# One decode kernel, four small edits at once: where the identity is built, the first POOL instruction, the row layout of two weights, and the last attention pair

## The chip, the cores and the metric

The kernel runs on one NeuronCore of a Trainium2 chip. The metric is the device time of one execution in microseconds (us). Times of the same kernel on the same chip differ by one to five microseconds from run to run, which is as much as the parts of this change are worth. So the study leans on two instruments: timed runs (five or six of each later kernel, means compared) and stretches inside the traces that are much steadier than the total.

## The reference, cut to what matters

Eight sequences decode one token through two layers. Each layer is attention with a cache of 4096 keys and values, then a small network. Of the first norm's "mixer" only the residual remains at sequence length 1, so B_w1 and B_w2 are never read.

```python
B, Sq, D = 8, 1, 448;  Hq, Hkv, Sk, Dh = 16, 8, 4096, 256;  F = 1792
def A(x, k_cache, v_cache, wq, wo):
    q = (x @ wq) -> [B, Hq, 1, Dh]
    scores = q @ k^T * Dh**-0.5          # each kv head serves 2 query heads
    o = softmax(scores) @ v
    return o.reshape(B, 1, Hq * Dh) @ wo
def Bl(x, ...):                          # what is left of it for S = 1
    return x + gelu(layernorm(x) @ w3) @ w4
x = A_x
for layer in range(2):                   # same weights and caches in both layers
    x = x + A(layernorm(x), ...)
    x = x + Bl(layernorm(x), ...)
```

The caches are 134 MB each. The kernel streams both in layer 1, and in layer 2 streams the values and those keys that it could not keep on the chip: 472 MB in all.

## The kernel before

Five buffers of 1 MB form a ring. SyncE issues one load when a buffer comes free. TensorE turns keys by a matmul with the identity, VectorE and ScalarE copy them out of PSUM (where matmuls leave their results), TensorE forms scores; POOL sums over partitions. A helper records every operation with what it reads and writes, so a line number in the profile is that of the call. Of a matmul's two operands the stationary one is loaded first and held (a weight load in the profile), and the moving one is streamed past it.

```python
# start: the identity, which every transpose needs
op("pool", lambda e: e.memset(ident[:, :], 0.0), writes=[r_ident])
op("pool", lambda e: e.affine_select(out=ident[:, :], in_=ident[:, :], compare_op=ALU.not_equal,
                                     fill=1.0, base=0, pattern=[[-1, P]], channel_multiplier=1), ...)
op("dve", lambda e: e.tensor_copy(ident4[:, :], ident[:, :]), ...)
...
# 448 rows = 3 chunks of 128 and one of 64: the 64 rows are stored as two half-width pieces,
# the lower columns on partitions 0-63, the upper on 64-127
def load_rows(t, tf, src, name):
    w = src.shape[1] // 2
    for kc in range(1, KC):
        parts.append((t[:, kc - 1, :], src[row0(kc):row0(kc + 1), :]))
    for half in range(2):
        parts.append((tf[64 * half:64 * half + 64, :], src[0:64, w * half:w * half + w]))
...
# wo (after the first pair) and w4: one 896-byte row to a partition and a packet
A_wo.rearrange("(t m) n -> m t n", m=P)
...
def pv(g, a):                             # probabilities times values, half a pair
    for i in range(HALF):                 # probabilities are the stationary operand (128 x 2)
        e.matmul(pvb[at:at + 2, 0:DH], pT[q][0][:, a * HALF + i, :], v[:, i, :], ...)
    if a == 1:
        op("dve", lambda e: e.tensor_copy(ob[:, :], pvb[:, 0:DH]), ...)
def finish(g):                            # turn the result: two transposes, a sum of 4 parts, a scale
    e.transpose(pvb[:, ...], ob[:, c * P:(c + 1) * P], ident4[:, :]) ...
    op("dve", tensor_reduce(os_, ...)); op("dve", tensor_tensor(oT[...], os_, 1 / sum, ALU.mult))
...
def rsqrt(src, dst, n):                   # integer first guess, three Newton steps: 11 VectorE operations
...
g = len(seq) - 1                          # the end
finish(g - 1); pv(g, 0); pv(g, 1); finish(g); drain()      # drain: output projection, norm, network
op("dve", lambda e: e.tensor_copy(xo[:, :, :], xT[:, :, :]), ...)
```

## Time and profile before

| | before |
|---|---|
| time, median of 3 runs | 1171.94 us |
| span of the profiled run | 1170.8 us |
| DMA queue of the kernel's loads | 98.4% of 16 engines' span |
| TensorE / VectorE / ScalarE / POOL busy | 80 / 42 / 27 / 9% |
| start of the last value matmuls to the end | 15.3 us |

From the page of the kernel before: the busy line of TensorE, the DMA share and the rate in 40 equal slices (tenths; GB/s), and the queue line (packets, MB, share).

```profile
PE 937.4 (80%) x19304; PEld 816.5 (70%) x19304; DVE 488.2 (42%) x1792; ACT 312.8 (27%) x891; POOL 105.4 (9%) x281
...
DMA  9999999999999999999999999999999999999994
GB/s 346 384 416 420 418 405 416 421 418 420 399 421 420 419 414 413 410 420 418 411 408 418 419 418 405 420 420 405 415 418 420 404 419 411 418 416 399 399 411 166
...
q1 hardware_dynamic: 70496, 471.97, 98.4%
```

DMA is busy in every slice but the last. The rate is about 420 GB/s where it is good, 346 and 384 in the first two slices (29 us each), and dips to around 400 in some later ones. A kernel like this has only two places where time can be won: stretches in which the stream is slow, and the work that is left when the last values have come.

The start, from the timeline of the kernel before (columns: start us, busy us, engine, line, operation, output and inputs, count, idle time before and what ended it).

```profile
11.19 0.28 POOL L204 TENSOR_SCALAR_AFFINE_SELECT ident<-ident 128x128 bf16<-128x128 bf16 x1 [10.27 <-issue]
...
11.84 5.86 PE L601 MATMUL tk<-ident,ring 128*128 128x128 f32 x32
...
21.35 0.44 POOL L350 PARTITION_ALL_REDUCE sg<-sm  x1 [9.87 <-issue]
...
22.25 0.26 PE L412 MATMUL mm<-lnT,wq_sb 128*128 128x24 bf16 x3 [4.56 <-DVE lnT L378]
```

POOL idles for 10.27 us before its first real instruction and 9.87 us before the first sum, with no other engine to blame ("issue"). The profile does not show what it waits for; the prediction takes it for a load of code, and "wait for code" below is this reading. Nothing can be transposed before 11.5 us.

The same trace by stretches (columns: stretch, length, busy time and count of TensorE, weight loads, VectorE, ScalarE, POOL, then granted clock, DMA share, GB/s; a share above 1 means that packets overlap).

```profile
11.00:15.00 4.00, 3.47 (x19) 3.44 (x20) 2.56 (x13) 0.59 (x1) 0.28 (x1) 1.00 1.02 432
15.00:19.00 4.00, 2.70 (x19) 2.46 (x17) 0.39 (x1) 1.76 (x3) 0.00 (x0) 1.00 1.09 247
32.00:41.00 9.00, 7.40 (x138) 6.56 (x138) 3.88 (x11) 3.76 (x10) 1.06 (x3) 1.00 1.09 380
```

At 11 to 15 us full-width loads move at 432 GB/s. From 15 to 19 us the rate is 247 at a DMA share of 1.09: the engines are not idle, each packet takes longer. At 32 to 41 us it is wo's turn, at 380.

The tail, from the timeline, cut to the steps that the change touches.

```profile
1155.49 1.02 PE L699 MATMUL pvb<-ring,pT 128*2 128x256 bf16 x16 [0.63 <-DMA ring<-in_A_v_cache_dram]
1156.57 0.42 DVE L705 COPY ob<-pvb 128x256 f32<-128x256 f32 x1 [3.94 <-PE pvb L699]
...
1157.05 0.69 PE L717 MATMUL pvb<-ident,ob 128*128 128x128 f32 x2 [0.53 <-DVE ob L705]
1157.78 0.17 DVE L720 TENSOR_REDUCE os<-pvb 128x4 f32<-128x16 f32 x1 [0.65 <-PE pvb L717]
1157.99 0.18 DVE L724 TENSOR_TENSOR oT<-os,rc 128x4 bf16<-128x4 f32 x1
...
1158.22 0.83 PE L451 MATMUL mm<-oT,wo_sb 128*64 128x24 bf16 x16 [0.48 <-DVE oT L724]
...
1161.91 0.17 DVE L327 TENSOR_SCALAR smi<-sm 128x6 int32<-128x6 int32 x1
...
1163.92 0.17 DVE L337 SCALAR_TENSOR_TENSOR sm<-sm 128x6 f32<-128x6 f32 x1
...
1164.90 0.24 ACT L496 ACTIVATE hw<-hw 128x42 f32<-128x42 f32 x1 [13.57 <-DVE hw L494]
...
1167.84 0.18 DVE L768 CAST xo<-xx 128x32 bf16<-128x32 f32 x1
...
1169.14 0.31 SPq L779 DMA_DIRECT2D out_dram<-x_row  x1
```

From the last landing (1155.49, read here and below as the start of the matmuls that wait for it) to the output projection (1158.22) are 2.73 us; the inverse root is 1161.91 to 1164.15, just before the network's hidden layer needs it.

### The profile page before, as it was taken

The numbers are of one execution on the slowest core, as the hardware profiler recorded it, in microseconds if no ns is written. First come the engines' busy times: TensorE is split into PE (matmuls) and PEld (weight loads), VectorE is DVE, ScalarE is ACT, GpSimd is POOL, SyncE is SP. The second block draws the span as 40 slices with busy tenths as digits, with TensorE's granted clock in tenths as the row PEclk, the third lists the DMA queues.
The fourth block names the chain that finished last, engine by engine and source line by source line (L and its number), as shares of the span: only waits on it lengthen the run. The fifth ranks groups of instructions, "written<-read, shape, count | busy, mean of one in ns | idle before, by whom it ended". The sixth has DMA issues, their size and how long they took to land.

```text
span 1170.8 us, 42672 instructions
## 1 busy us (share of the span) xinstructions
PE 937.4 (80%) x19304; PEld 816.5 (70%) x19304; DVE 488.2 (42%) x1792; ACT 312.8 (27%) x891; POOL 105.4 (9%) x281
## 2 busy tenths in 40 slices
PE   4777898779877887778877888778887888889986
PEld 3666776668766776667766777667776777778774
DVE  2324543345334543345334543345333633354343
ACT  1223222223223232232223222223222322222230
POOL 0000001101010010000100010001000011000100
PEclk8879999999999999899989998999999999999996
DMA  9999999999999999999999999999999999999994
GB/s 346 384 416 420 418 405 416 421 418 420 399 421 420 419 414 413 410 420 418 411 408 418 419 418 405 420 420 405 415 418 420 404 419 411 418 416 399 399 411 166
DMA packets 70678, 474.70 MB, mean 405 GB/s; under 512 B 7248, under 2 KB 13280, under 8 KB 13792
## 3 DMA queue, kind: packets, MB, share of 16 engines
q1 hardware_dynamic: 70496, 471.97, 98.4%
q8 instruction: 151, 2.47, 0.9%
q14 instruction: 31, 0.25, 0.1%
HBM read 471.93 MB, written 0.01 MB: 403 GB/s over the span
## 4 chain that ended last, share of the span: by engine, by line
DMA 54%; PE 33%; DVE 8%; issue 4%; ACT 1%; POOL 1%; SPq 0%; POOLq 0%; DVEq 0%; ACTq 0%
DMA ring<-in_A_k_cache_dram 53%; PE tk L601 15%; PE ps L625 6%; PE pvb L699 5%; PE mm L451 3%; DVE ktr L608 2%; PE mm L412 1%; DMA ring<-in_A_v_cache_dram 1%; PE mm L515 1%; PE pvb L717 1%; DVE oT L724 1%; POOL gm L675 1%; DVE os L720 1%; DVE keep L608 1%; DVE ob L705 0%
## 5 line engine op out<-in xcount | busy, mean ns | idle before, releaser
L601 PE MATMUL tk<-ident,ring 128*128 128x128 f32 x2944 | 407.0, 290 | 138.8 <-DMA ring<-in_A_k_cache_dram 138.5
L601 PEld LDWEIGHTS tk<-ident,ring 128*128 128x128 f32 x2944 | 342.7, 148 | 184.7 <-DMA ring<-in_A_k_cache_dram 177.7
L608 DVE COPY ktr<-tk 128x512 f32<-128x512 f32 x224 | 153.9, 690 | 198.5 <-PE tk L601 198.1
L606 ACT COPY ktr<-tk 128x512 f32<-128x512 f32 x224 | 130.0, 586 | 310.1 <-PE tk L601 309.7
L699 PE MATMUL pvb<-ring,pT 128*2 128x256 bf16 x4096 | 160.0, 277 | 32.7 <-DMA ring<-in_A_v_cache_dram 23.9
L625 PE MATMUL ps<-qT,keep 128*128 128x48 bf16 x4608 | 160.2, 185 | 6.3 <-issue 3.8
L608 DVE COPY keep<-tk 128x512 f32<-128x512 f32 x144 | 99.5, 691 | 143.2 <-PE tk L601 141.9
L625 PEld LDWEIGHTS ps<-qT,keep 128*128 128x128 bf16 x4608 | 146.0, 98 | 16.1 <-issue 8.9
L606 ACT COPY keep<-tk 128x512 f32<-128x512 f32 x144 | 84.3, 586 | 257.1 <-PE tk L601 257.1
L681 ACT ACTIVATE pT<-ps,nb 128x32 bf16<-128x32 f32 x256 | 76.6, 299 | 260.0 <-DVE nb L677 213.2
L625 PE MATMUL ps<-qT,ktr 128*128 128x48 bf16 x3584 | 129.8, 183 | 10.0 <-ACT ktr L606 6.2
L625 PEld LDWEIGHTS ps<-qT,ktr 128*128 128x128 bf16 x3584 | 115.7, 97 | 20.6 <-ACT ktr L606 8.4
L675 POOL PARTITION_ALL_REDUCE gm<-pm x128 | 45.8, 357 | 782.7 <-DVE pm L672 782.7
L699 PEld LDWEIGHTS pvb<-ring,pT 128*2 128x2 bf16 x4096 | 76.2, 82 | 56.0 <-DMA ring<-in_A_v_cache_dram 28.5
L451 PE MATMUL mm<-oT,wo_sb 128*128 128x24 bf16 (+1 forms) x1408 | 64.1, 187 | 14.4 <-DVE oT L724 4.8
L705 DVE COPY ob<-pvb 128x256 f32<-128x256 f32 x128 | 53.8, 420 | 41.1 <-PE pvb L699 40.7
L451 PEld LDWEIGHTS mm<-oT,wo_sb 128*128 128x128 bf16 (+1 forms) x1408 | 51.5, 101 | 27.2 <-DVE oT L724 19.9
L686 POOL PARTITION_ALL_REDUCE dn<-rs x128 | 51.3, 401 | 151.0 <-ACT pT L681 151.0
L672 DVE TENSOR_REDUCE pm<-ps 128x2 f32<-128x64 f32 x128 | 28.7, 224 | 74.7 <-PE ps L625 74.1
L717 PE MATMUL pvb<-ident,ob 128*128 128x128 f32 x256 | 53.1, 290 | 6.9 <-DVE ob L705 6.9
L412 PE MATMUL mm<-lnT,wq_sb 128*128 128x24 bf16 x864 | 47.8, 184 | 5.2 <-DVE lnT L378 4.6
L412 PEld LDWEIGHTS mm<-lnT,wq_sb 128*128 128x128 bf16 x864 | 39.4, 98 | 14.8 <-issue 6.4
(68 smaller groups left out, 479.0 us busy)
## 6 DMA issues: line engine op xcount, KB each, us to landing
ring<-in_A_v_cache_dram SPq DMA_DIRECT2D x256, 1024.0 KB, 10.3
ring<-in_A_k_cache_dram SPq DMA_DIRECT2D x184, 1024.0 KB, 10.7
wo_sb<-in_A_wo_dram SPq DMA_DIRECT2D x1, 3584.0 KB, 25.0
wq_sb<-in_A_wq_dram SPq DMA_DIRECT2D x3, 1024.0 KB, 11.7
w_sb<-in_B_w_dram SPq DMA_DIRECT2D x1, 1568.0 KB, 18.2
w_sb<-in_B_w_dram SPq DMA_DIRECT2D x3, 448.0 KB, 16.0
wqf_sb<-in_A_wq_dram SPq DMA_DIRECT2D x2, 256.0 KB, 15.5
w3f_sb<-in_B_w_dram SPq DMA_DIRECT2D x2, 112.0 KB, 16.2
```

Of the source, the lines that this page charges most:

```text
L412: last = e.matmul(room(P, at + t * B, n), cols(kc, t), copies(rhs, n), start=(kc == 1), stop=(kc == 0), skip_group_check=True)
L451: last = e.matmul(room(w, C_P + c, 1), wo[:, t, row0(c):row0(c) + w], copies(oT[:, t // 2, t % 2, b:b + 1], 1), start=(t == 4 * h), stop=( ...
L601: last = e.transpose(bank[:, j * P:(j + 1) * P], src[:, 4 * (f % 4) + j, :].bitcast(f32), ident4[:, :])
L606: op("act", lambda e: e.copy(flat, bank[:, :]), reads=[r_bank], writes=[r_kt])
L608: op("dve", lambda e: e.tensor_copy(flat, bank[:, :]), reads=[r_bank], writes=[r_kt])
L625: last = e.matmul(pst[:, at:at + 2 * N_REP].rearrange("p (r j) -> p r j", j=2), kt(i, c), repeated(qT[:, b, c, 2 * h:2 * h + 2]), start=(c ...
L675: op("pool", lambda e: e.partition_all_reduce(gm[q][0][:, :], pm[q][0][:, :], P, ReduceOp.max), reads=[pm[q][1]], writes=[gm[q][1]])
L681: return e.activation(pT[q][0][:, :, :].rearrange("p i j -> p j i")[:, j, :], pst[:, C_S:C_S + 2 * NI].rearrange("p (i j) -> p j i", j=2)[ ...
L686: op("pool", lambda e: e.partition_all_reduce(dn[q][0][:, :], rs[q][0][:, :], P, ReduceOp.add), reads=[rs[q][1]], writes=[dn[q][1]])
L699: last = e.matmul(pvb[at:at + 2, 0:DH], pT[q][0][:, a * HALF + i, :], v[:, i, :], start=(a == 0 and i < 4), stop=(a == 1 and i >= HALF - 4 ...
L705: op("dve", lambda e: e.tensor_copy(ob[:, :], pvb[:, 0:DH]), reads=[r_pv], writes=[r_ob])
L717: last = e.transpose(pvb[:, DH + c * P:DH + (c + 1) * P], ob[:, c * P:(c + 1) * P], ident4[:, :])
```

## The change

Four edits. Identity: VectorE counts 0 to 31, turns that block and compares the two. POOL: its first instruction is a sum over partitions of zeros, so that the wait before POOL's first sum is over before a sum is needed. Rows: wo and w4 are stored with two consecutive rows on one partition (1792-byte packets); the columns of w3 and the order of the heads' elements follow (w3's 64 rows are now cut at column 1024, not 896), and wo is queued at the start. Tail: for the last pair the values are the stationary operand, so the result comes out already turned; the last 1 MB load is cut in two; the last inverse root is ScalarE's square root with its table loaded ahead; the result is written to the output tile directly.

```diff
-    op("pool", lambda e: e.memset(ident[:, :], 0.0), ...)
-    op("pool", lambda e: e.affine_select(out=ident[:, :], ...), ...)
-    op("dve", lambda e: e.tensor_copy(ident4[:, :], ident[:, :]), ...)
+    op("pool", lambda e: e.memset(sg[:, :], 0.0), writes=[r_sg])
+    op("pool", lambda e: e.partition_all_reduce(sg[:, :], sg[:, :], P, ReduceOp.add), ...)
+    for w in (1, 2, 4, 8, 16):                                   # count 0..31
+        op("dve", ... tensor_single_scalar(count[:, w:2 * w], count[:, 0:w], float(w), ALU.add), ...)
+    op("dve", lambda e: e.transpose(rows_, count), ...)
+    for p in range(0, P, 32):
+        op("dve", ... tensor_tensor(ident4[p:p+32, p:p+32], rows_[p:p+32], count[p:p+32], ALU.is_equal), ...)
...
-        lambda: op("sp", ... wo[:, :, :], A_wo.rearrange("(t m) n -> m t n", m=P) ...)    # after the first pair
+    op("sp", lambda e: e.dma_start(paired(wo), rows_of(A_wo)), ...)                       # at the start
+    def paired(t):   return t[:, :, :].rearrange("p (u c) n -> p u (c n)", c=2)
+    def rows_of(src): return src.rearrange("(u p c) n -> p u (c n)", p=P, c=2)
...
+        pieces = [(0, HALF, r)] if n < len(chunks) - 1 else [(0, HALF // 2, r), (HALF // 2, HALF, r_end)]
...
+    def rsqrt_end(src, dst, n):
+        op("act", lambda e: e.activation(w, v, ACT.Sqrt), ...)
+        table(ACT.Tanh)                       # a one-column activation that pulls the table back
+        op("dve", reciprocal) ... three more VectorE operations (one Newton step)
...
+    def close(g):
+        table(ACT.Sqrt)
+        for lo, hi in ((0, HALF), (HALF, HALF + HALF // 2), (HALF + HALF // 2, NI)):
+            for i in range(lo, hi):
+                for c in range(2):            # values stationary (128 x 128), probabilities moving
+                    e.matmul(tk[c][0][:, 0:48], v[:, i % HALF, c::2], repeated(pT[q][0][:, i, :]), ...)
+        for c in range(2):
+            op("dve", ... tensor_tensor(oT[:, 2*h:2*h+2, c, b], tk[c][0][:, 0:2], rc[q][0][:, :], ALU.mult), ...)
...
-    finish(g - 1); pv(g, 0); pv(g, 1); finish(g)
+    finish(len(seq) - 2)
+    while side: step()
+    close(len(seq) - 1)
...
-    op("dve", lambda e: e.tensor_copy(xo[:, :, :], xT[:, :, :]), ...)
+        to, r_to = (x_, r_x) if layer == 0 else (xo[:, :, lo:lo + n], r_xo)
```

More of the change, by code (lines that the diff above doesn't have):

```diff
@@ L15 @@
 NF = F // P
+F_LOW = 1024
 LN_EPS = 1e-5
@@ L151, in decode_two_layers @@
     w3, r_w3 = sb("w3_sb", [P, KC - 1, F], bf)
-    w3f = nc.alloc_sbuf_tensor("w3f_sb", [P, F // 2], bf)
+    w3f = nc.alloc_sbuf_tensor("w3f_sb", [P, F_LOW], bf)
     w4, r_w4 = sb("w4_sb", [P, NF, D], bf)
@@ L171, in decode_two_layers @@
     r_lift = Res()
+    r_table = Res()
     sm, r_sm = sb("sm", [P, 8, 2 * B], f32)
@@ L200, in decode_two_layers @@
     C_P = 448
-    op("pool", lambda e: e.memset(ident[:, :], 0.0), writes=[r_ident])
-    op("pool", lambda e: e.affine_select(out=ident[:, :], in_=ident[:, :],
-                                         compare_op=ALU.not_equal, fill=1.0, base=0,
-                                         pattern=[[-1, P]], channel_multiplier=1),
-       reads=[r_ident], writes=[r_ident])
-    op("dve", lambda e: e.tensor_copy(ident4[:, :], ident[:, :]), reads=[r_ident], writes=[r_ident4])
+    op("pool", lambda e: e.memset(sg[:, :], 0.0), writes=[r_sg])
+    op("pool", lambda e: e.partition_all_reduce(sg[:, :], sg[:, :], P, ReduceOp.add), reads=[r_sg], writes=[r_sg])
+    count, r_count = xc[:, :, :].rearrange("p c b -> p (c b)"), r_xc
+    rows_, r_rows = t1[:, :, :].rearrange("p c b -> p (c b)"), r_t1
+    op("dve", lambda e: e.memset(count[:, 0:1], 0.0), writes=[r_count])
+    op("dve", lambda e: e.memset(ident4[:, :], 0.0), writes=[r_ident4])
+    for w in (1, 2, 4, 8, 16):
+        op("dve", lambda e, w=w: e.tensor_single_scalar(count[:, w:2 * w], count[:, 0:w], float(w), ALU.add),
+           reads=[r_count], writes=[r_count])
+    op("dve", lambda e: e.transpose(rows_, count), reads=[r_count], writes=[r_rows])
+    for p in range(0, P, 32):
+        op("dve", lambda e, p=p: e.tensor_tensor(ident4[p:p + 32, p:p + 32], rows_[p:p + 32], count[p:p + 32],
+                                                 ALU.is_equal),
+           reads=[r_count, r_rows], writes=[r_ident4])
+    op("dve", lambda e: e.tensor_copy(ident[:, :], ident4[:, :]), reads=[r_ident4], writes=[r_ident])
     op("dve", lambda e: e.memset(pvb[:, :], 0.0), writes=[r_pv])
+    r_w3f = Res()
+    op("dve", lambda e: e.memset(w3f[64:P, F - F_LOW:F_LOW], 0.0), writes=[r_w3f])
     op("dve", lambda e: e.memset(xx[:, :, :, :], 0.0), writes=[r_x])
@@ L271, in decode_two_layers @@
     state = {"loaded": 0}
+    r_end = Res()
     def load_next():
@@ L279, in load_next, with load_rows @@
         t, r = ring[n % N_RING]
-        op("sp", lambda e: e.dma_start(
-            t[:, :, :], src[b, h].rearrange("(m s) d -> m s d", m=P)[:, a * HALF:(a + 1) * HALF, :]),
-           writes=[r], dma=f"ring{n % N_RING}")
+        pieces = [(0, HALF, r)] if n < len(chunks) - 1 else [(0, HALF // 2, r), (HALF // 2, HALF, r_end)]
+        r_end.w, r_end.r = r.w, list(r.r)
+        for k, (lo, hi, r_) in enumerate(pieces):
+            op("sp", lambda e, lo=lo, hi=hi: e.dma_start(
+                t[:, lo:hi, :], src[b, h].rearrange("(m s) d -> m s d", m=P)[:, a * HALF + lo:a * HALF + hi, :]),
+               writes=[r_], dma=f"ring{n % N_RING}" if k == 0 else "end")
     def row0(kc):
         return max(0, kc * P - 64)
-    def load_rows(t, tf, src, name):
+    def load_rows(t, tf, src, name, low):
         parts = []
-        w = src.shape[1] // 2
         for kc in range(1, KC):
             parts.append((t[:, kc - 1, :], src[row0(kc):row0(kc + 1), :]))
-        for half in range(2):
-            parts.append((tf[64 * half:64 * half + 64, :], src[0:64, w * half:w * half + w]))
+        parts.append((tf[0:64, 0:low], src[0:64, 0:low]))
+        parts.append((tf[64:P, 0:src.shape[1] - low], src[0:64, low:]))
         return [op("sp", lambda e, o=o, i=i: e.dma_start(o, i), writes=[Res()], dma=f"{name}{k}")
@@ L303, in reads_of, with paired, rows_of @@
         return out_
+    def paired(t):
+        return t[:, :, :].rearrange("p (u c) n -> p u (c n)", c=2)
+    def rows_of(src):
+        return src.rearrange("(u p c) n -> p u (c n)", p=P, c=2)
     op("sp", lambda e: e.dma_start(x_row[:, :], A_x[:, 0, :]), writes=[r_row], dma="x")
@@ L307, in decode_two_layers, with table @@
     load_next()
-    wq_r = reads_of(load_rows(wq, wqf, A_wq, "wq"))
+    wq_r = reads_of(load_rows(wq, wqf, A_wq, "wq", HQ * DH // 2))
     for _ in range(2, N_RING):
         load_next()
+    op("sp", lambda e: e.dma_start(paired(wo), rows_of(A_wo)), writes=[r_wo], dma="wo")
     late = [
-        lambda: op("sp", lambda e: e.dma_start(wo[:, :, :], A_wo.rearrange("(t m) n -> m t n", m=P)),
-                   writes=[r_wo], dma="wo"),
-        lambda: w3_r.extend(reads_of(load_rows(w3, w3f, B_w3, "w3"))),
-        lambda: op("sp", lambda e: e.dma_start(w4[:, :, :], B_w4.rearrange("(t m) n -> m t n", m=P)),
+        lambda: w3_r.extend(reads_of(load_rows(w3, w3f, B_w3, "w3", F_LOW))),
+        lambda: op("sp", lambda e: e.dma_start(paired(w4), rows_of(B_w4)),
                    writes=[r_w4], dma="w4"),
     ]
-    w3_r = []
+    w3_r = [r_w3f]
     def bc(t, n):
         return t.unsqueeze(1).to_broadcast([P, KC, n])
+    def table(f):
+        op("act", lambda e: e.activation(sm[:, 5, 0:1], ident4[:, 0:1], f), reads=[r_ident4], writes=[r_table])
+    def rsqrt_end(src, dst, n):
+        v, y, w = sm[:, src, 0:n], sm[:, dst, 0:n], sm[:, 7, 0:n]
+        op("act", lambda e: e.activation(w, v, ACT.Sqrt), reads=[r_sm], writes=[r_sm])
+        table(ACT.Tanh)
+        op("dve", lambda e: e.reciprocal(y, w), reads=[r_sm], writes=[r_sm])
+        op("dve", lambda e: e.tensor_tensor(w, y, y, ALU.mult), reads=[r_sm], writes=[r_sm])
+        op("dve", lambda e: e.scalar_tensor_tensor(w, w, -0.5, v, ALU.mult, ALU.mult), reads=[r_sm], writes=[r_sm])
+        op("dve", lambda e: e.scalar_tensor_tensor(y, w, 1.5, y, ALU.add, ALU.mult), reads=[r_sm], writes=[r_sm])
+        yield
     def rsqrt(src, dst, n):
@@ L339, in rsqrt, with layernorm @@
             yield
-    def layernorm(lo, n, twice):
+    def layernorm(lo, n, twice, end=False):
         x_ = xT[:, :, lo:lo + n]
@@ L372, in layernorm @@
         yield
-        yield from rsqrt(2, 3, 2 * n if twice else n)
+        yield from (rsqrt_end if end else rsqrt)(2, 3, 2 * n if twice else n)
     def centered(dst, r_dst, lo, n):
@@ L400, in w3_cols @@
     def w3_cols(kc, t):
-        if kc > 0:
-            return w3[:, kc - 1, t * P:(t + 1) * P]
-        return w3f[:, t % (NF // 2) * P:(t % (NF // 2) + 1) * P]
+        cols = w3[:, kc - 1, :] if kc > 0 else w3f[:, :]
+        u = t // 2 % (NF // 2 if kc > 0 else F_LOW // 256)
+        return cols[:, 256 * u:256 * u + 256].rearrange("p (m c) -> p c m", c=2)[:, t % 2, :]
     def project(cols, r_w, at, ts, upper, n):
@@ L475, in outputs, with mix @@
            reads=[r_mm, r_x], writes=[r_x])
-    def mix(lo, n):
+    def mix(lo, n, layer=0, end=False):
         y_ = mm[:, C_Y:C_Y + KC * B].rearrange("p (c n) -> p c n", n=B)[:, :, lo:lo + n]
         x_ = xT[:, :, lo:lo + n]
-        yield from layernorm(lo, n, True)
+        yield from layernorm(lo, n, True, end)
         for _ in range(WAIT):
             yield
-        for ts in (range(0, 2), range(2, 4), range(4, 7), range(7, 9), range(9, 11), range(11, 14)):
-            project(w3_cols, w3_r, C_H, ts, ts[0] >= NF // 2, n)
+        for ts in (range(0, 2), range(2, 4), range(4, 6), range(6, 8), range(8, 11), range(11, 14)):
+            project(w3_cols, w3_r, C_H, ts, ts[0] >= F_LOW // P, n)
             yield
@@ L519, in mix @@
             yield
-        op("dve", lambda e: e.scalar_tensor_tensor(x_, y_, 0.5, xres[:, :, 0:n], ALU.mult, ALU.add),
-           reads=[r_mm, r_xres], writes=[r_x])
+        to, r_to = (x_, r_x) if layer == 0 else (xo[:, :, lo:lo + n], r_xo)
+        op("dve", lambda e: e.scalar_tensor_tensor(to, y_, 0.5, xres[:, :, 0:n], ALU.mult, ALU.add),
+           reads=[r_mm, r_xres], writes=[r_to])
         yield
@@ L716, in fn @@
             for c in range(2):
-                last = e.transpose(pvb[:, DH + c * P:DH + (c + 1) * P], ob[:, c * P:(c + 1) * P], ident4[:, :])
+                last = e.transpose(pvb[:, DH + c * P:DH + (c + 1) * P],
+                                   ob[:, :].rearrange("p (m c) -> p c m", c=2)[:, c, :], ident4[:, :])
             return last
@@ L727, in finish, with fn @@
            reads=[r_os, rc[q][1]], writes=[r_o[b]])
+        after(g)
+    def close(g):
+        layer, b, h = seq[g]
+        q = g % N_PS
+        table(ACT.Sqrt)
+        op("dve", lambda e: e.reciprocal(rc[q][0][:, :], dn[q][0][:, :]), reads=[dn[q][1]], writes=[rc[q][1]])
+        for lo, hi in ((0, HALF), (HALF, HALF + HALF // 2), (HALF + HALF // 2, NI)):
+            v, r_v = ring[index["v", g, lo // HALF] % N_RING]
+            def fn(e, lo=lo, hi=hi, v=v):
+                last = None
+                for i in range(lo, hi):
+                    for c in range(2):
+                        last = e.matmul(tk[c][0][:, 0:2 * N_REP].rearrange("p (r j) -> p r j", j=2),
+                                        v[:, i % HALF, :].rearrange("p (m c) -> p c m", c=2)[:, c, :],
+                                        repeated(pT[q][0][:, i, :]), start=(i == 0), stop=(i == NI - 1),
+                                        skip_group_check=True)
+                return last
+            op("pe", fn, reads=[r_end if hi == NI else r_v, pT[q][1]], writes=[tk[0][1], tk[1][1]])
+        for c in range(2):
+            op("dve", lambda e, c=c: e.tensor_tensor(oT[:, 2 * h:2 * h + 2, c, b], tk[c][0][:, 0:2], rc[q][0][:, :],
+                                                     ALU.mult),
+               reads=[tk[c][1], rc[q][1]], writes=[r_o[b]])
         after(g)
@@ L743, in after @@
         elif b == N_ONCE - 1:
-            jobs.extend([outputs(0, N_ONCE), mix(0, N_ONCE)])
+            jobs.extend([outputs(0, N_ONCE), mix(0, N_ONCE, 1)])
         elif g == len(seq) - 1:
-            jobs.append(mix(N_ONCE, B - N_ONCE))
+            jobs.append(mix(N_ONCE, B - N_ONCE, 1, True))
     jobs.append(queries(0, B))
@@ L759, in decode_two_layers @@
             late.pop(0)()
-    g = len(seq) - 1
-    finish(g - 1)
-    pv(g, 0)
-    pv(g, 1)
-    finish(g)
+    finish(len(seq) - 2)
+    while side:
+        step()
+    close(len(seq) - 1)
     drain()
-    op("dve", lambda e: e.tensor_copy(xo[:, :, :], xT[:, :, :]), reads=[r_x], writes=[r_xo])
     def f_o(e):
```

## The prediction

> **What bounds the kernel.** The DMA queue does. The page shows it at 98.4% of the 16 engines' span, 9 tenths in every slice but the last, 471.97 MB; PE is at 80%, DVE at 42%. In the windows view the rate is about 419 GB/s nearly everywhere. Data flows from about 2.5 us to 1154.5 us. So only two things can move the time: DMA inefficiency, and the serial tail after the last value chunk lands (first dependent matmul at 1155.49, end at 1170.8: 15.3 us).
>
> **The start: large in compute, about 0 us in time.** The timeline shows POOL idle for 10.27 us before the affine select and 9.87 us before the first all-reduce, both ended by "issue". The Trainium skill, "GPSIMD Engine Reference", Instruction dispatch, says the first call of a freshly loaded kernel pays an invisible code load (about 6 us there; here about 10 us, twice). After the change there is one, hidden under the weight loads: key transposes start near 5 us instead of 11.83, the first layernorm sum near 11.5 instead of 21.35. But projection also needs the wq rows, whose last packets end near 19 us, so it starts near 19.5 instead of 22.25. Through all of this the DMA engines are busy (share about 1.0 from 2 us on): 9 MB are queued before the first buffer has to come free. Earlier compute only frees buffers that DMA cannot fill sooner. The slow stretches at 15 to 20 us and 54 to 58 us (148 to 307 GB/s) coincide with the 64-partition loads of wq and w3, which stay.
>
> **Row packing: about -1.0 us.** In the trace's packet records an 896-byte packet took 41.4 ns, an 8192-byte one 317.6 ns. A straight line through them (estimate) gives 75.3 ns for 1792 bytes. wo and w4 are 368 small packets per engine: 15.2 us before, 184 x 75.3 = 13.9 us after. Packets overlap there (share 1.09), so I count 1.0 of the 1.4 us.
>
> **The tail: about -2.3 us.**
> - Values as stationary operand. Before: landing at 1155.49, 16 matmuls 1.02, copy 0.42, transposes 0.69, reduce 0.17, multiply 0.18 with handoffs: output projection at 1158.22, 2.73 us after landing. After: the last half chunk needs 16 matmuls, 0.83 us if like the projection's 16 at this slow clock, then two multiplies of 0.18: about 1.3 us. Gain 1.4.
> - Square root. The integer/Newton chain takes 1161.91 to 1164.15, 2.24 us. After: one ACT instruction (0.22), four DVE of 0.20, handoffs: 1.1 us. The table back to tanh must load meanwhile: the one load in the trace takes 1.28 us plus a dummy activation 0.2, and tanh is wanted about 1.58 us after the square root, so it just fits. The Trainium skill, "ScalarE: Activation LUTs", What ACT_TABLE_LOAD costs, adds about 1.38 us of drain per switch; this trace shows none. If it is paid, the gain vanishes. Expected 0.7.
> - The removed copy into the output tile: 0.2.
>
> **Prediction: 1168.6 us, 80% range 1166.6 to 1170.6. Faster by over 2%: 0.02; within 2%: 0.97; slower by over 2%: 0.01.**
>
> **Checks.** Timeline: one POOL wait of about 10 us; transposes from about 5 us; DMA rate in the first 60 us unchanged except during wo and w4; last landing about 1 us earlier; landing to output projection 1.3 us; DVE or ACT idle before tanh tells the table's price; landing to end about 13 us.
>
> **What would make it wrong.** A table drain ahead of tanh (+1.1 us); early compute filling DMA gaps I did not see (-2 us or more); strided weight reads on PE slower than 100 ns; different buffer-release timing adding or removing the dips, such as 331 GB/s at 1105 us.

## The result, and the profile after

The changed kernel took 1169.38 us (median of 4 runs, 1168.58 to 1169.43) beside 1171.83 (1171.44 to 1172.33) for the kernel before. The ratio is 0.9977, with a 95% interval of 0.9960 to 0.9995. A ratio here is the mean time of one kernel's runs over that of the other's of the same rounds, so it is not quite the ratio of the medians. Two further sets gave 0.9959 and 0.9967. Over all later sets the kernel before has a mean of 1172.9 us (38 runs on four chips, means per chip 1172.3 to 1173.2), the changed kernel 1168.8 (11 runs on two chips): 4.1 us, with a 95% interval of about 0.7 from the spread of the runs. The first set's 2.45 was the smallest of three.

The rate line and the queue line of the page after:

```profile
GB/s 352 386 419 420 418 401 420 420 418 416 404 420 420 417 405 420 414 421 415 400 422 419 417 404 412 419 420 406 417 420 419 407 418 411 421 419 397 400 401 219
...
q1 hardware_dynamic: 67696, 471.97, 98.7%
```

The start after, from the timeline:

```profile
0.96 0.48 POOL L207 PARTITION_ALL_REDUCE sg<-sg  x1
...
6.37 6.27 PE L643 MATMUL tk<-ident,ring 128*128 128x128 f32 x32 [2.68 <-DMA ring<-in_A_k_cache_dram]
...
8.70 0.45 POOL L391 PARTITION_ALL_REDUCE sg<-sm  x1 [7.26 <-DVE sm L387]
...
19.50 0.23 PE L453 MATMUL mm<-lnT,wq_sb 128*128 128x24 bf16 x3 [6.86 <-DMA wqf_sb<-in_A_wq_dram]
```

The transposes moved from 11.84 to 6.37 us, where a landing holds them, and the first layernorm sum from 21.35 to 8.70, where VectorE holds it. POOL waits for no code at all now, not even once. The projection moved only from 22.25 to 19.50, because it needs the wq rows.

The stretches after (wo is queued earlier, so its turn is 26 to 35 us):

```profile
11.00:15.00 4.00, 1.64 (x12) 1.40 (x10) 3.09 (x14) 1.17 (x2) 0.00 (x0) 1.00 1.01 426
15.00:19.00 4.00, 0.00 (x0) 0.00 (x0) 0.00 (x0) 0.00 (x0) 0.00 (x0) 0.51 1.04 287
26.00:35.00 9.00, 7.99 (x126) 7.20 (x122) 3.47 (x8) 3.10 (x8) 1.15 (x3) 0.85 1.06 382
```

Full-width loads are as fast as before; the slow stretch is a little less slow (287 against 247 GB/s); wo moves at 382 against 380, although its packets are twice as large.

The tail after:

```profile
1151.94 2.08 PE L786 MATMUL tk<-pT,ring 128*128 128x48 bf16 x48
...
1154.36 0.82 PE L786 MATMUL tk<-pT,ring 128*128 128x48 bf16 x16 [0.34 <-DMA ring<-in_A_v_cache_dram]
1155.22 0.37 DVE L793 TENSOR_TENSOR oT<-tk,rc 128x2 bf16<-128x2 f32 x2 [2.85 <-PE tk L786]
...
1155.64 0.72 PE L492 MATMUL mm<-oT,wo_sb 128*64 128x24 bf16 x16 [0.46 <-DVE oT L793]
...
1159.22 0.21 ACT L357 ACTIVATE sm<-sm 128x6 f32<-128x6 f32 x1 [7.69 <-DVE sm L411]
...
1159.44 1.28 ACT L352 ACT_TABLE_LOAD   x1
1159.46 0.19 DVE L359 RECIPROCAL sm<-sm 128x6 f32<-128x6 f32 x1 [0.27 <-ACT sm L357]
...
1160.08 0.17 DVE L362 SCALAR_TENSOR_TENSOR sm<-sm 128x6 f32<-128x6 f32 x1
...
1160.74 0.20 ACT L352 ACTIVATE sm<-ident 128x1 f32<-128x1 f32 x1
...
1161.06 0.24 ACT L537 ACTIVATE hw<-hw 128x42 f32<-128x42 f32 x1
...
1163.80 0.18 DVE L562 SCALAR_TENSOR_TENSOR xo<-mm,xres 128x12 bf16<-128x12 f32 x1 [1.59 <-PE mm L556]
...
1165.09 0.31 SPq L844 DMA_DIRECT2D out_dram<-x_row  x1
```

Three quarters of the values are done before the last landing, and 1.28 us after it (1154.36 to 1155.64) the output projection starts: 1.45 less than before. The root takes 1159.22 to about 1160.26, 1.04 instead of 2.24. The table comes back in 1.28 us beside VectorE; the dummy activation ends at 1160.94 and tanh waits for VectorE until 1161.06. Last landing to end is 12.4 us instead of 15.3. That is the clearest number: 12.2 to 12.6 us in all twelve traces with the new tail, 15.3 in both with the old.

The two traces differ by 4.0 us of span, 2.9 of them in the tail. The last landing is 1.1 us earlier, but landings of one and the same program vary by more than that (1154.36, 1156.48 and 1154.74 in three traces of the changed kernel), so the first pair of traces cannot say whether start and rows paid.

### The profile page after: what moved, and what is told of

It reads as the page before. It is cut to its first block, busy times and chain, and to the rows that moved or that the text cites. A ratio compares the mean times of both kernels' runs of the same rounds, so it can differ in the third digit from the quotient of the medians.

```text
span 1166.8 us, 42740 instructions
## 1 busy us (share of the span) xinstructions
PE 949.8 (81%) x19334; PEld 829.4 (71%) x19334; DVE 489.4 (42%) x1796; ACT 316.1 (27%) x896; POOL 107.2 (9%) x281
## 4 chain that ended last, share of the span: by engine, by line
DMA 49%; PE 37%; DVE 8%; issue 3%; ACT 1%; POOL 1%; SPq 0%; POOLq 0%; DVEq 0%; ACTq 0%
DMA ring<-in_A_k_cache_dram 48%; PE tk L643 16%; PE ps L667 7%; PE pvb L741 5%; PE mm L492 3%; DVE ktr L650 3%; PE mm L453 2%; PE mm L556 1%; DMA wqf_sb<-in_A_wq_dram 1%; PE pvb L759 1%; DVE oT L767 1%; DVE os L763 1%; POOL gm L717 1%; DVE keep L650 0%; DVE ob L747 0%
## 5 line engine op out<-in xcount | busy, mean ns | idle before, releaser
L643 PE MATMUL tk<-ident,ring 128*128 128x128 f32 x2944 | 412.4, 293 | 134.2 <-DMA ring<-in_A_k_cache_dram 133.1
L643 PEld LDWEIGHTS tk<-ident,ring 128*128 128x128 f32 x2944 | 347.0, 150 | 179.9 <-DMA ring<-in_A_k_cache_dram 168.9
L759 PE MATMUL pvb<-ident,ob 128*128 128x128 f32 x254 | 58.1, 311 | 6.4 <-DVE ob L747 6.4
L714 DVE TENSOR_REDUCE pm<-ps 128x2 f32<-128x64 f32 x128 | 28.6, 224 | 75.7 <-PE ps L667 75.3
```

The source lines that it names most:

```text
L643: last = e.transpose(bank[:, j * P:(j + 1) * P], src[:, 4 * (f % 4) + j, :].bitcast(f32), ident4[:, :])
L759: last = e.transpose(pvb[:, DH + c * P:DH + (c + 1) * P], ob[:, :].rearrange("p (m c) -> p c m", c=2)[:, c, :], ident4[:, :])
```

## The experiments

Each kernel below is the changed kernel with one edit. The kernels of one set ran on the same chip in the same rounds as the kernel before. "Against the changed kernel" compares means with its 11 later runs (1168.8); the intervals are 95%, from the spread of the runs (1.96 standard errors, about a tenth too narrow for so few runs). Only the sets on two chips, 10 and 2, hold the changed kernel; the kernel before differs by up to 0.9 us between chips, so the ratio column has to agree. To place a gain inside the stream, I also read from each trace's packet records when the first 8.5 MB had arrived, that is, when the wq rows and most of the first caches were in, and when 30 MB had (all weights in).

| run | median us | ratio to before | against the changed kernel | 8.5 MB at | 30 MB at |
|---|---|---|---|---|---|
| after_again, after_2 | 1168.07, 1169.10 | 0.9959, 0.9967 | - | 25.1, 24.6 | 78.7, 78.5 |
| tail_old | 1172.07 | 0.9990 | +3.5 ± 0.8 | 24.7 | 78.7 |
| start_old, start_old_2 | 1170.29, 1169.61 | 0.9972, 0.9974 | +1.2 ± 0.8 | 25.3, 25.6 | 79.1, 79.5 |
| no_early_sum | 1168.81 | 0.9966 | +0.3 ± 1.0 | 24.6 | 78.4 |
| pool_both | 1168.90 | 0.9966 | +0.3 ± 1.0 | 24.6 | 78.4 |
| fetch_only | 1169.50 | 0.9974 | +1.1 ± 1.0 | 25.2 | 79.1 |
| rows_single | 1169.25 | 0.9966 | +0.6 ± 1.1 | 24.9 | 78.7 |
| rows_eight (wrong layout) | 1167.61 | 0.9966 | -0.6 ± 1.1 | 24.6 | 77.2 |
| full_ports (wrong layout) | 1166.77 | 0.9946 | -2.3 ± 0.9 | 23.4 | 76.1 |
| alt_skew | 1168.82 | 0.9966 | 0.0 ± 0.9 | 23.8 | 77.3 |

The first traces gave 25.7 and 80.0 (before), 24.9 and 79.1 (after). Between the two marks the kernel before took 54.4 us, the three traces of the changed kernel 53.6 to 54.2 and rows_single 53.8. So up to about half a microsecond may belong to wo's earlier place or to w3's new cut, which no run undid alone. All twelve runs passed the comparison with the reference, even the two with rows in the wrong places. The weights' share of the result is small beside the comparison's tolerance, so that comparison is no proof of the weights' layout.

### The changed kernel again (after_again)

No edit.

> The changed kernel once more, as the measure of noise. If the whole gain is the tail (2.85 us in the two traces) the time is 2.9 us under the kernel before; if the earlier end of the value stream in the first trace (1.1 us) belongs to the change as well, 4.0 us under. Landing to end 12.5 us either way.

Measured: 1168.07 us, ratio 0.9959 (0.9944 to 0.9974), 4.7 us by means in this set and 4.0 in the second; landing to end 12.4 us. The larger of the two expected numbers holds over 11 runs, so more than the tail pays. The spread of the runs (1167.69 to 1170.71) shows why single runs were not enough.

### The tail undone (tail_old)

```diff
-    close(len(seq) - 1)
+    pv(g, 0); pv(g, 1); finish(g)                    # g = last pair; the last load whole again
-        yield from (rsqrt_end if end else rsqrt)(2, 3, ...)
+        yield from rsqrt(2, 3, ...)
-        to, r_to = (x_, r_x) if layer == 0 else (xo[...], r_xo)
+        to, r_to = x_, r_x                            # and the copy into xo back
```

> Only the tail is undone (last pair as all others, integer square root, copy into the output tile). Theory A, the gain is the tail: 2.85 us slower than the changed kernel, landing to end 15.3 us, and equal to the kernel before within 0.5 us. Theory B, start and row packing also pay about 1 us: 2.85 us slower than the changed kernel, but 1 us faster than the kernel before.

From the timeline of this kernel, the last value matmuls and the store that ends the program:

```profile
1155.76 1.02 PE L741 MATMUL pvb<-ring,pT 128*2 128x256 bf16 x16 [1.53 <-DMA ring<-in_A_v_cache_dram]
...
1169.41 0.31 SPq L846 DMA_DIRECT2D out_dram<-x_row  x1
```

Measured: the span ends at 1171.1, so landing to end is 15.3 us again, 2.9 more. The timed difference, 3.5 ± 0.8, holds that. Against the kernel before it is 0.6 to 0.9 us faster (ratio 0.9990, interval 0.9975 to 1.0005), which fits theory B's 1 us better than A's equality but excludes neither by itself.

### The start undone (start_old, and again as start_old_2)

```diff
-    op("pool", ... memset(sg)); op("pool", ... partition_all_reduce(sg, sg))
-    ... identity on VectorE ...
+    op("pool", ... memset(ident)); op("pool", ... affine_select(ident)); op("dve", ... tensor_copy(ident4, ident))
```

> Only the start is undone (identity by the POOL affine select, no early POOL sum). My theory, the DMA queue hides it: time within 0.4 us of the changed kernel, although the first transposes go from 6.4 back to about 11.8 us and the first layernorm sum from 8.7 to about 21 us. Rival, the earlier start is what moved the stream 0.7 us ahead at 15 to 20 us in the first trace: 0.7 us slower.

Measured: 1.2 us slower than the changed kernel over both sets of each (11 runs against 11, interval 0.5 to 2.0). My theory falls. The stream is 0.2 to 1.0 us later already at 8.5 MB, and stays that much later at 30 MB.

### The two parts of the start (after_2, no_early_sum, pool_both, start_old_2)

A two by two table on one chip.

```diff
 no_early_sum:
-    op("pool", ... memset(sg)); op("pool", ... partition_all_reduce(sg, sg))
 pool_both:
     op("pool", ... memset(sg)); op("pool", ... partition_all_reduce(sg, sg))
-    ... identity on VectorE ...
+    op("pool", ... memset(ident)); op("pool", ... affine_select(ident)); op("dve", ... tensor_copy(ident4, ident))
```

> The changed kernel a third time, now as one corner of a two by two table (identity on VectorE or by affine select; early POOL sum or not) on one chip. In the last set undoing both cost 1.6 us of the mean, where I had expected at most 0.4. Theory A (queue hides the start, the 1.6 us was chance): all four corners within 0.6 us. Theory B (earlier compute does pay): the corner with neither is 1 to 2 us slower than this one.

> Identity on VectorE, no early POOL sum. Of the code load: if the first all-reduce of a program always costs about 10 us of fetching, the first layernorm sum moves from 8.7 to beyond 18 us; if only the second library pays (the affine select's and then its replacement), it stays at 8.7 us and the early sum is worth nothing. Of the time: theory A within 0.6 us of the changed kernel, theory B slower only if the sum comes late enough to hold up the projection, which the wq rows release at 19.5 us.

> Early POOL sum, then the identity by affine select. If each change of POOL code costs about 10 us, the affine select ends near 11 us and the layernorm sum near 21 us, as in the kernel before, so this corner must equal the corner with neither: theory A within 0.6 us of the changed kernel, theory B 1 to 2 us slower.

> Neither part of the new start, repeated. Theory A: within 0.6 us of the changed kernel. Theory B: 1 to 2 us slower again, together with the corner that has the early sum and the affine select.

POOL's instructions in the timeline with both (early sum, then affine select), and then without the early sum and with the identity on VectorE:

```profile
0.97 0.48 POOL L207 PARTITION_ALL_REDUCE sg<-sg  x1
...
1.77 0.29 POOL L209 TENSOR_SCALAR_AFFINE_SELECT ident<-ident 128x128 bf16<-128x128 bf16 x1 [0.16 <-POOL ident L208]
...
8.73 0.45 POOL L383 PARTITION_ALL_REDUCE sg<-sm  x1 [6.67 <-DVE sm L379]
```

```profile
8.72 0.48 POOL L389 PARTITION_ALL_REDUCE sg<-sm  x1 [8.29 <-DVE sm L385]
```

After a sum the affine select runs at once (1.77 us, idle 0.16 for its memset) and the next sum waits only for its input. The sum alone, first used at 8.72 us, waits only for its input too. So neither the sum nor the affine select costs 10 us as such: both waits appear only where the affine select is the first of them. Either half of the new start removes both waits, and doing both is belt and braces. The times follow: 1169.10, 1168.81 and 1168.90 for the three corners without the waits, 1169.61 for the one with them. By means that is 0.9 us, too little for this chip's five runs each to show alone. Taking all 21 runs without the waits against the 11 with them gives 1.1 ± 0.7 us. My expectation that the corner with both would equal the corner with neither was wrong, for the reason just given.

### Only the wait for code put back (fetch_only)

```diff
-    op("pool", ... memset(sg)); op("pool", ... partition_all_reduce(sg, sg))
+    op("pool", ... memset(ob)); op("pool", ... affine_select(ob))       # an unused tile; identity stays on VectorE
```

> The changed kernel, but POOL begins with an affine select on an unused tile in place of the early sum; the identity stays on VectorE. So POOL waits about 10 us twice as in the kernel before, and the layernorm sum comes near 20 us, but the transposes stay at 6.4 us. What slows the 64-partition loads of wq (98th percentile minus 2nd: 3.2 to 3.5 us where the affine select is POOL's first work, 2.4 to 2.9 us elsewhere)? Theory fetch: the second wait for POOL code overlaps them; then 3.3 us here. Rival, the late transposes and their copies overlap them; then 2.6 us here.

POOL in the timeline of this kernel, and its stretch from 15 to 19 us:

```profile
11.37 0.28 POOL L207 TENSOR_SCALAR_AFFINE_SELECT ob<-ob 128x128 f32<-128x128 f32 x1 [10.44 <-issue]
...
21.62 0.44 POOL L394 PARTITION_ALL_REDUCE sg<-sm  x1 [9.97 <-issue]
```

```profile
15.00:19.00 4.00, 0.00 (x0) 0.00 (x0) 0.00 (x0) 0.00 (x0) 0.00 (x0) 0.59 1.04 256
```

Measured: 1.1 ± 1.0 us slower than the changed kernel (nearer ± 1.1 for so few runs, so the time alone does not settle it), 8.5 MB at 25.2 us, 30 MB at 79.1: like the kernels with the old start, although its transposes begin at 6.27 us. In the stretch no compute engine did anything (all busy times 0.00), and the stream moved 256 GB/s; the changed kernel's three traces have 287, 254 and 309 there. So the loss does not need the late transposes; what goes with it is the wait for POOL's code. The duration of the wq pieces, which I had named as the measure, came out at 2.95 us, between the two numbers, and decides nothing by itself. Taking the traces with the affine select first (before, start_old, start_old_2, fetch_only), 8.5 MB arrive at 25.2 to 25.7 us; in the eight others with the same wq rows they arrive at 24.6 to 25.1, on average 0.7 us sooner. The rates at 15 to 19 us are 247 to 266 and 254 to 309, so they overlap. The packet records say where the loss arises: 5 MB are in at 14.9 to 15.3 us in all twelve, 6.5 MB at 20.45 to 20.98 in the four and at 19.75 to 20.26 in the eight. The loads up to 8.9 MB had all been issued by 7.1 us, so buffers that come free later cannot be the reason. How such a wait slows the stream is open: the profile counts no bytes for it, and while it went on at 11 to 15 us full-width loads moved at 428 GB/s.

### Single rows in the same places (rows_single)

```diff
-    op("sp", ... dma_start(paired(wo), rows_of(A_wo)))                   # packets of 1792 bytes
+    for c in range(2):                                                   # two loads, packets of 896 bytes
+        op("sp", ... dma_start(wo "p (u c) n -> p c u n"[:, c], A_wo "(u p c) n -> p c u n"[:, c]))
     (w4 likewise)
```

> Same placement of wo and w4, but loaded as two transfers of single 896-byte rows each. My prediction's size: 1.0 us slower. From the packet times of both traces (368 packets of 41.4 ns against 184 of 79.1 ns per engine): 0.7 us slower. Rival, the stream's progress in the two traces shows 0.2 us over that stretch: no difference that can be seen.

Measured: 1169.25 us, 0.6 ± 1.1 slower than the changed kernel, which excludes neither 0 nor the predicted 1.0. The stream speaks for no difference: 30 MB are in at 78.7 us here and in after_again, from the same chip. The rates stand with the next run.

### Rows of eight and seven, a wrong layout on purpose (rows_eight)

```diff
-    rows_of(src): "(u p c) n -> p u (c n)", c=2
+    c=8 for wo, c=7 for w4                                               # packets of 7168 and 6272 bytes
```

> Wrong result on purpose: wo with eight and w4 with seven consecutive rows on a partition, so packets of 7168 and 6272 bytes (wider than the model's 256-wide heads allow). Single rows (896 bytes) moved at 378 GB/s during wo, pairs (1792 bytes) at 381, the 8192-byte cache rows move at about 420. If row size is what holds wo down, and pairs are just too small a step, wo now runs at 410 or more and its 3.67 MB take 0.8 us less than with pairs, w4 0.3 us less. If something else about wo holds it down (where it lies, its pattern in the tile), it stays near 381.

wo's stretch with single rows, and then with eight:

```profile
26.00:35.00 9.00, 7.39 (x121) 6.71 (x119) 3.55 (x8) 3.56 (x12) 1.15 (x3) 0.91 1.09 378
```

```profile
25.50:34.00 8.50, 8.18 (x136) 7.50 (x133) 3.16 (x6) 3.06 (x8) 0.79 (x2) 0.82 1.01 419
```

A single row took 41.1 ns a packet, a pair 79.1, eight rows 276.6. So pairs need 96% of the packet time of two singles, but in the stream that shows as 378 against 382 GB/s: over wo's 3.67 MB a tenth of a microsecond (9.71 against 9.61 us). At 30 MB the trace with single rows is where the others are (78.7). Eight rows reach 419, and 30 MB arrive 1.3 us sooner, more than the 1.1 expected. The time does not show it (-0.6 ± 1.1 on another chip; the ratio, 0.9966, is like the changed kernel's 0.9959 and 0.9967). So row size is what holds wo down, and two rows are too small a step to be felt. Eight cannot be had in this layout, because with 256 elements to a head more than two rows on each of 128 partitions would mix heads.

### The 64-partition loads as full-width loads, a wrong layout on purpose (full_ports)

```diff
-        parts.append((tf[0:64, 0:low], src[0:64, 0:low]))
-        parts.append((tf[64:P, 0:src.shape[1] - low], src[0:64, low:]))
+        half = src.shape[1] // 2
+        parts.append((tf[:, 0:half], src[0:64, :].rearrange("r (t c) -> (r t) c", t=2)))
```

> Wrong result on purpose: the last 64 rows of wq and w3 are loaded as one transfer each over all 128 partitions, same bytes, rows in wrong places. If the slow stretches at 15 to 19 us and 43 to 47 us come from loads that fill only 64 partitions at a time, they vanish (rate near 420 GB/s) and the kernel is about 2.5 us faster than the changed one. If they come from something else there at that time, no change.

The result stands with that of the next run.

### The same loads in turns of 16 rows (alt_skew)

```diff
-        parts.append((tf[0:64, 0:low], src[0:64, 0:low]))
-        parts.append((tf[64:P, 0:src.shape[1] - low], src[0:64, low:]))
+        high_rows(0, 32, 4)                           # 8 rows to partitions 64, 68, ..., 92
+        for b in range(4):
+            low_rows(b, 64, 4)                        # 16 rows to partitions b, b + 4, ...
+            high_rows(*((b + 1, 64, 4) if b < 3 else (32, 64, 4)))
```

> Correct result. The two 64-partition loads of wq and of w3 are cut into transfers of 16 rows, lower and upper partitions in turn, with 8 rows of the upper ones first[...]. If the half-filled partitions are the cause and the order spreads them, about half of what the full-width load gains: 1 to 1.5 us faster than the changed kernel. If small transfers cost more than that, slower.

The stretch from 15 to 19 us with full width, and then with turns:

```profile
15.00:19.00 4.00, 1.35 (x51) 1.39 (x52) 0.00 (x0) 0.00 (x0) 0.00 (x0) 0.66 1.02 426
```

```profile
15.00:19.00 4.00, 0.12 (x5) 0.15 (x6) 0.00 (x0) 0.00 (x0) 0.00 (x0) 0.64 1.04 370
```

With full width the slow stretch is gone (426 GB/s), and so is that of w3 (43 to 47 us: 282 GB/s in the changed kernel, 416 here). The same 4096-byte packets took 159 ns, where the three traces of the changed kernel have means of 246 to 289, and the kernel is 2.3 ± 0.9 us faster (1166.77 us). So the 64-partition loads themselves are the cause of the slow stretches. The Trainium skill, "DMA: Bandwidth & Descriptors", The descriptor swizzle, says that in a full transfer engines 0 to 7 write the ports of partitions 0 to 63 and engines 8 to 15 those of 64 to 127. Sixteen engines on half the partitions would then have half the ports, which fits packets that take 1.5 to 1.8 times as long; no run here shows ports.

Turns bring 370 GB/s and put the stream 1.2 us ahead at 30 MB (2.4 us with full width; both against after_2's 78.5). Yet the time, 1168.82, is the changed kernel's. Its trace shows the lead shrinking late: 470 MB are in at 1147.8 us, as in after_2, while full_ports keeps more than a microsecond (1145.9). One trace of each is weak evidence: the three of the changed kernel range from 1147.8 to 1150.4 there. With an interval of 0.9 us this run neither shows a gain nor excludes one near 0.9. So no kernel here is shown to be both correct and faster than the changed one.

## Why the prediction was right or wrong

The total was right: 1168.6 us predicted, 1169.38 measured, inside the range, and 1168.8 as the mean of 11 later runs. Within it the gain of the rows was put 0.9 us too high, that of the tail 0.6 and that of the start 0.7 to 1.1 too low. That these errors offset each other is luck, and so is part of the hit.

- What bounds the kernel: right. Every gain found lies either in a slow stretch of the stream or after the last landing.
- The tail, "about -2.3 us": right in mechanism, undersized. The trace shows 2.9. The value matmuls gave 1.45 for a predicted 1.4. The root gave 1.2 where I had discounted 1.1 to 0.7 for the table. The copy into the output tile gave 0.2 as predicted. The Trainium skill, "ScalarE: Activation LUTs", What ACT_TABLE_LOAD costs, adds about 1.38 us of drain to the load's 1.28; here the next activation started 0.02 us after the load ended (1160.74 after 1159.44 plus 1.28), so the discount was for nothing. The trace before could not have told: after its only table load ScalarE had nothing to do for 11.84 us. Undoing the tail cost 3.5 ± 0.8. The three parts were not undone one by one; their sizes are read from the traces.
- "Row packing: about -1.0 us": wrong. The step that failed is the straight line through packet times, 75.3 ns for 1792 bytes where 79.1 were measured, and then reading a sum of packet times as stream time: with 79.1 the same sum gives 0.7 instead of 1.4. The stretch shows 0.1 us, and undoing it 0.6 ± 1.1.
- "The start: large in compute, about 0 us in time": wrong in the second half. Undoing it cost 1.2 ± 0.8. The compute did move as told (transposes at 6.37 for near 5, projection at 19.50 for 19.5), and as told that was hidden: fetch_only has the early transposes and still loses. What I left out is that the stream loses about 0.7 us where POOL waits for code (seen in all four traces with such waits; how is open), within the stretch that I had called unchanged.
- "After the change there is one" wait for code: wrong. There is none (first sum at 0.96 us, next at 8.70).
- "The slow stretches ... coincide with the 64-partition loads": right, and full_ports makes it the cause.

The terms as measured, 2.9 for the tail, 0.7 to 1.1 for the start and 0.1 for the rows, add up to 3.7 to 4.1 us, and the later sets show 4.1 ± 0.7. What sets the run-to-run difference of one to five microseconds, and what gives back part of an early lead in the last tenth of the run, stays open. In the traces it lies in dips of the rate, of about 1 us each, in differing places.

## What to carry to other kernels

When a queue is saturated, cost an edit by what it does to the queue's rate, and check the trace for slow stretches in which the engines are busy; a load that fills only half of the partitions ran in stretches of 60 to 75% of the full rate here, and that was worth more than packing rows. The order in which POOL first used its instructions cost 20 us of waiting here, and one instruction moved ahead removed it. In this serial tail every step removed counted in full, and it can be read from one trace; effects on the stream of less than 1 us need many runs.

## What the Trainium skill lacked or had wrong

- "GPSIMD Engine Reference", Instruction dispatch: it gives one invisible code load of about 6 us at the first call of a freshly loaded kernel. Here there were two waits of about 10 us (10.27 and 9.87) when the affine select came before the all-reduce, and none when the all-reduce came first, for either instruction (affine select at 1.77 us). The page says nothing of the order. No page says that the stream loses about 0.7 us beside such waits.
- "ScalarE: Activation LUTs", What ACT_TABLE_LOAD costs: the load's 1283 ns agree (1.28 us), the drain of about 1380 ns does not show: the next activation began 0.02 us after each of the two loads in the tail (1151.33 after 1150.03 plus 1.28, and 1160.74).
- "DMA: Bandwidth & Descriptors", Rules for kernel authors: it says of two transfers to disjoint partition halves only that they serialize and that one full transfer is better. Here one full transfer was better: 4096-byte packets took 246 to 309 ns to half the partitions (means of a trace) and 159 ns to all. It lacks the case of the two halves cut into turns of 16 rows: these ran at 370 GB/s, where the two whole transfers had 247 to 309.
- "DMA: Bandwidth & Descriptors", Specifications: it gives 512 bytes as the least transfer for line rate. Here 896-byte rows moved at 378 GB/s, 1792-byte rows at 382, 7168-byte rows at 419.
